# Layer 1's activations stored as they are, and turned by the loads that use them

## The chip, the cores and the metric

The kernel runs on one core of a Trainium2 chip. The metric is the device time of one execution in microseconds (us). Seven executions of the kernel before took 740.19 to 762.38 us, with a median of 745.99 us. The core has a matrix engine (TensorE: PE, its weight loads PEld), a vector engine (DVE), a scalar engine (ACT), a general engine (GpSimd: POOL), a queue processor (SyncE: SP) and 16 DMA engines, which all queues share. SP issues most transfers and takes its instructions in order; POOL issues others, among them most stores.

## The reference

The program computes a network of four blocks, A B A B, and all its gradients. A is a gated long convolution over the sequence, B a two-layer perceptron, each on a layernorm of its input with a residual around it; both A blocks and both B blocks share weights.

```python
def _B_ref(x, w1, w2):                       # S, D, F = 2048, 448, 1792
    h = jnp.einsum("bsd,df->bsf", x, w1)
    h = _silu(h)
    return jnp.einsum("bsf,fd->bsd", h, w2)

x = A_q
x = x + _A_ref(_layernorm(x), A_k, A_v, A_shift_k, A_ssm_k, A_ssm_D)
x = x + _B_ref(_layernorm(x), B_w1, B_w2)    # layer 1
x = x + _A_ref(_layernorm(x), A_k, A_v, A_shift_k, A_ssm_k, A_ssm_D)
x = x + _B_ref(_layernorm(x), B_w1, B_w2)    # layer 2
out, vjp = jax.vjp(f, A_q, A_k, A_v, A_shift_k, A_ssm_k, A_ssm_D, B_w1, B_w2)
return (out, *vjp(grad_out))
```

What matters here is the gradient of w2. It is the sum over both layers of a product over the sequence: activation (silu of h, 1792 features by 2048 positions) times the gradient that reaches the layer's output (2048 positions by 448).

## The kernel before, in words

The work has four stages, read from the trace's lines.

- **Prefix** (0 to about 100 us): the convolution of block A by a matrix form of the Fourier transform.
- **Main** (about 100 to 515 us), in chunks of 512 positions, four a layer. Layer 1 forward (to about 230 us); layer 2 forward and backward together (to about 400 us); layer 1 backward (to about 515 us).
- **Suffix** (about 515 us to the end): the backward convolution. It consists of small matmuls with vector work between them.
- **Weight-gradient jobs.** The gradients of w2 (`_gw2`) and w1 (`_gw1`) are cut into 14 blocks of 128 features each. A block is two jobs, one a layer, of 16 matmuls each (one for 128 positions), which add into one PSUM tile. A job (`_job`) first loads 128 features by 2048 positions (512 KB) into a tile dstat, in which 128 positions lie on the partitions. The jobs have no dependence on the work beside them, so their matmuls are put between other matmuls in a fixed order: `fill` does it in the layer-1 backward (about four jobs), `weave` in the suffix. Five buffers of dstat rotate (three in the layer-1 backward); a load is issued when the job that had the buffer is done.

In the forward, `h` computes a half chunk (7 of 14 feature blocks) of the hidden layer with features on the partitions: four PSUM groups, of which ACT writes silu to a tile aT and DVE or ACT a copy to dT. The tag of aT has three buffers: the aT of a half takes the buffer of the half three before it, and waits until everything that reads that one is done. `out` reads aT for the second matmul.

The w2 jobs need the activation turned, with positions on the partitions. Before the change this is done as follows.

- Layer 1, first half of a chunk: `store_turned` issues two transposing transfers on SP from aT into a tile "turned" (two buffers), 16 and 12 blocks of 128 by 128. The next call's `flush` issues the store of "turned" to A_d[0] in HBM.
- Layer 1, second half: blocks 4 to 6 of its seven likewise (12 blocks of 128 by 128). Blocks 0 to 3 go to AP_d untouched, by a store on POOL.
- Layer 2: both halves are turned and stored to A_d[1]. Besides, `turn_plain` in chunks 0 and 1 loads AP_d's four feature blocks back with a transposing transfer and stores them to A_d[0].
- The weights w2T and w1T, needed in the backward, are made by six transposing loads ("pieces"). From the fourth call of `store_turned` on, each call issues one behind its own transposes.
- The jobs of w2 then load from A_d[0] and A_d[1] with plain transfers (L891). The jobs of w1 load layer 2's part from GH_d, which was turned, and layer 1's part from GP_d, which was stored untouched, with a transposing load (L889).

The order of instructions on an engine comes from a scheduler, with places pinned by `issue_after`, `_in_turn` and `keep_in_program_order`. In the suffix, three transposing transfers on SP turn a part of the Fourier data (Zg<-A1g, L992); each is issued after the job load before it.

Lines that the prediction uses: L536 matmuls of `contract` (h and the backward's gh); L628 ACT's silu to aT; L113 a copy by DVE; L505 transposes of `store_turned`; L509 pieces; L512 and L523 stores to A_d; L522 `turn_plain`; L639 and L642 POOL's stores of dT and to AP_d; L889 and L891 loads of a job, L893 its matmuls; L1006 and L205 loads of kk_c and Minvs on POOL; L1148 small matmuls near the end.

Of the kernel before, what the change touches and what calls it, by code (L numbers as in the profile page):

```python
# [17 lines left out]
P = 128  # L18
# [4 lines left out]
NT = 16  # L23
# [97 lines left out]
def kernel(  # L121
# [36 lines left out]
    k.DT_d = dram.tile([4, 2, P, NF // 2, 512], BF16, name="DT_d")  # L158
    k.A_d = [dram.tile([P, NF, NT, P], BF16, name=f"A_d{i}") for i in range(2)]
    k.AP_d = dram.tile([4, P, S], BF16, name="AP_d")  # L160
    k.GH_d = dram.tile([P, NF, NT, P], BF16, name="GH_d")
# [36 lines left out]
    _ssm_suffix(k)  # L198


W2_PLAIN = (7, 8, 9, 10)

# [279 lines left out]
class Main:  # L482

    def __init__(self, k, es):
        self.k, self.nc, self.tc = k, k.nc, k.tc
        nc, tc = k.nc, k.tc
        pool = lambda name, **kw: es.enter_context(tc.tile_pool(name=name, bufs=1, reuse_waits="tile", **kw))
        self.wt = pool("mwt")
        self.w2T = self.wt.tile([P, ND, F], BF16, name="w2T")
        self.w1T = self.wt.tile([P, NF, D], BF16, name="w1T")  # L490
        self.td = pool("mtd")
        self.ch = pool("mch")
        self.X = k.X
        self.late = None
        self.turns = 0
        self.pieces = [(self.w2T[:, a:b, :], k.B_w2[:, lo:hi]) for a, b, lo, hi in ((0, 2, 0, 256), (2, 3, 256, 384), (3, 4, 320, 448))]
        self.pieces += [(self.w1T[:, a:b, :], k.B_w1[:, a * P:b * P]) for a, b in ((0, 5), (5, 10), (10, NF))]
        self.w1sb, self.w2sb, self.Y = k.w1sb, k.w2sb, k.Ysb

    def store_turned(self, dst, tile_, c, hh, groups=((0, 4), (4, 7))):  # L500
        nc = self.nc
        self.flush()
        an = self.td.tile([P, NF // 2, 4, P], BF16, name="turned", tag="S", bufs=2)
        for lo, hi in groups:
            nc.sync.dma_start_transpose(out=an[:, lo:hi].rearrange("p a t f -> p (a t) f"), in_=tile_[:, lo:hi, :].rearrange("p a s -> p (a s)"))  # L505
        self.turns += 1
        if self.turns > 3 and self.pieces:
            out, src = self.pieces.pop(0)
            i = nc.sync.dma_start_transpose(out=out, in_=src)  # L509
            self.tc.keep_in_program_order(i)  # L510
        lo, hi = groups[0][0], groups[-1][1]
        self.late = lambda: nc.sync.dma_start(out=dst[:, 7 * hh + lo:7 * hh + hi, 4 * c:4 * c + 4, :], in_=an[:, lo:hi])  # L512

    def flush(self):
        if self.late:
            self.late()
        self.late = None

    def turn_plain(self, i):
        an = self.td.tile([P, NT, P], BF16, name="turned", tag="S", bufs=2)  # L520
        self.flush()
        self.nc.sync.dma_start_transpose(out=an[:], in_=self.k.AP_d[i])  # L522
        self.late = lambda: self.nc.sync.dma_start(out=self.k.A_d[0][:, W2_PLAIN[i]], in_=an[:])  # L523

# [91 lines left out]
    def h(self, c, L, nT, half, hold, pre=None):  # L616
# [16 lines left out]
        if L == 1:  # L633
            if half == 1:
                with self.tc.issue_after(last.ins):
                    for _, d in hold:
                        self.slope(d)
        else:
            nc.gpsimd.dma_start(out=k.DT_d[c, half], in_=dT[:])  # L639
            self.store_turned(k.A_d[0], aT, c, half, ((0, 4), (4, 7)) if half == 0 else ((4, 7),))  # L640
            if half == 1:
                nc.gpsimd.dma_start(out=k.AP_d[:, :, 512 * c:512 * (c + 1)].rearrange("ft f s -> f ft s"), in_=aT[:, 0:4, :])  # L642
        if L == 1:
            self.store_turned(k.A_d[1], aT, c, half)
        return d0
# [26 lines left out]
    def ga(self, c, L, gT, dT, mid=None, loads=(None, None)):  # L672
# [3 lines left out]
        for fp in range(NF // 2):  # L676
# [15 lines left out]
            if fp in (3, 6):  # L692
# [3 lines left out]
                if L == 1:  # L696
                    self.store_turned(k.GH_d, ghT[hh], c, hh)
                else:
                    self.flush()
                    nc.gpsimd.dma_start(out=k.GP_d[7 * hh:7 * hh + 7, :, 512 * c:512 * (c + 1)].rearrange("ft f s -> f ft s"), in_=ghT[hh][:])  # L700
        return (ghT, *ld) if ld else ghT
# [74 lines left out]
    def run(self):  # L776
# [30 lines left out]
        for c in range(4):  # L807
# [4 lines left out]
            self.out(c, cur, True)  # L812
            if c < 2:
                self.turn_plain(2 * c)
                self.turn_plain(2 * c + 1)
            if c < 3:
# [64 lines left out]

def _job(k, ps, src, ft, mov, slot, start, stop, first=None):
    pl, tag, bufs = slot
    st = pl.tile([P, NT, P], BF16, name="dstat", tag=tag, bufs=bufs)
    with ExitStack() as es:
        if first is not None:
            es.enter_context(k.tc.issue_after(first))
        if src is None:
            k.job_load = k.nc.sync.dma_start_transpose(out=st[:], in_=k.GP_d[ft]).ins  # L889
        else:  # L890
            k.job_load = k.nc.sync.dma_start(out=st[:], in_=src[:, ft, :, :]).ins  # L891
# [5 lines left out]
def _gw2(k, pool, fts, slots, bufs=2, first=None):  # L897
    nc = k.nc
    for ft in fts:
        ps = k.psum.tile([P, 512], FP32, name="ps_d", tag="tr", bufs=2)  # L900
        for L, mov in ((0, k.X), (1, k.GO)):
            slot = slots.pop(0)
            slots.append(slot)
            yield from _job(k, ps, k.A_d[L], ft, mov, slot, L == 0, L == 1, first)
        o = pool.tile([P, D], BF16, name="dout", tag="dout", bufs=bufs)
# [4 lines left out]
def _gw1(k, pool, slots):  # L910
# [288 lines left out]
```

## Time and profile before

| what | value |
|---|---|
| median of 7 executions (lowest, highest) | 745.99 us (740.19, 762.38) |
| the profiled execution, and its span | 745.99 us, 744.2 us |
| granted TensorE clock, mean of the span | 0.993 |
| PE busy in the span; idle in 100:130, 130:160, 160:200, 200:400 | 697.5 us (94%); 2.3, 0.6, 3.3, 5.8 us |
| DMA engines, busy share in 100:130, 130:160, 160:200, 524:538, 538:558 | 0.78, 1.10, 1.13, 0.94, 1.11 |
| queue of SP (q1) | 112.71 MB, 63.2% of 16 engines' span |
| queue of POOL (q0) | 61.52 MB, 24.5% |
| turned<-aT, transposing, 28 times | median 6.4 us from issue to landing |
| dstat<-A_d, plain, 28 times | 5.2 us |
| dstat<-GP_d, transposing, 14 times | 7.1 us |

How to read it: all times on the page and in the trace are those of one profiled execution. A busy share of the DMA engines can pass 1, as packets overlap. "Landing" is the moment at which all 16 engines have reported a transfer done. A name like dstat<-A_d is the tile written and the one read. SP's time is that of issuing; a transposing transfer holds SP longer than a plain one, and longer still when the queues are full. In a list of waits, "A <- B" says that A's engine stood idle until B was done. The granted clock is the part of full speed that TensorE was given.

### The profile page before, as it was taken

To read this page: it belongs to the slowest core of one execution; us is meant where nothing else is said; L and a number is where in the kernel's file an instruction comes from. 1 tells how busy PE (TensorE), PEld (TensorE's weight loads), DVE (VectorE), ACT (ScalarE), POOL (GpSimd) and SP (SyncE) were. 2 spreads that over 40 slices of the span, in tenths; PEclk is the share of its full clock that TensorE was granted. 3 is DMA by queue.
4 is the path that set the end of the run, shared out by engine and by line. 5 is a ranking of instruction groups with operands and counts; after the bars stand their busy time and mean duration, and the time that the engine had idled before them with its cause. 6 is when DMAs were issued, how large, how long until landed. Compare 5 with 4: busy or idle time off the path is not lost.

```text
span 744.2 us, 12447 instructions
## 1 busy us (share of the span) xinstructions
PE 697.5 (94%) x4836; PEld 370.4 (50%) x4881; DVE 508.9 (68%) x1059; ACT 438.1 (59%) x555; POOL 118.5 (16%) x202
## 2 busy tenths in 40 slices
PE   6978789999899999999999999999999999999897
PEld 5866533444344443443434434434556667554453
DVE  4878888788633597885958979779218773697150
ACT  4688777666537578587686777755426675321001
POOL 1144222221100001000000100110201112233131
PEclk9999999999999999999999999999999999999999
DMA  9979959999999999888979845735896887999993
GB/s 312 235 191 273 358 186 240 214 289 238 287 221 256 210 204 276 196 219 187 229 197 272 300 180 208 288 108 172 295 291 251 319 314 237 306 251 220 216 222 72
DMA packets 200599, 177.55 MB, mean 239 GB/s; under 512 B 155162, under 2 KB 176734, under 8 KB 199388
## 3 DMA queue, kind: packets, MB, share of 16 engines
q1 hardware_dynamic: 184608, 112.71, 63.2%
q0 software_dynamic: 15008, 61.52, 24.5%
q10 hardware_dynamic: 924, 2.52, 1.0%
q8 instruction: 38, 0.62, 0.4%
q14 instruction: 21, 0.17, 0.1%
HBM read 69.32 MB, written 65.87 MB: 182 GB/s over the span
## 4 chain that ended last, share of the span: by engine, by line
PE 54%; DVE 16%; ACT 11%; DMA 10%; issue 4%; another core or an unknown queue 2%; SPq 1%; POOL 1%; ACTq 0%; DVEq 0%; POOLq 0%
PE ps_d L893 19%; PE ps_h L536 9%; PE ps_o L653 5%; PE ps_g L536 5%; PE ps_n L732 4%; DMA KB<-Z 4%; DMA turned<-aT 3%; DVE lb_junk L707 3%; DVE lb_u L718 2%; ACT nb L280 2%; PE ps_v L234 2%; PE ps_v L235 2%; ACT aT L628 1%; DVE dT L113 1%
## 5 line engine op out<-in xcount | busy, mean ns | idle before, releaser
L893 PEld LDWEIGHTS <-dstat 128*128 128x128 bf16 x896 | 85.3, 98 | 79.3 <-issue 4.5
L536 PE MATMUL ps_h<-nT,w1sb 128*128 128x512 bf16 (+1 forms) x432 | 103.6, 388 | 6.9 <-DVE dT L113 3.8
L536 PE MATMUL ps_g<-gT,w2T 128*128 128x512 bf16 (+1 forms) x432 | 94.3, 381 | 4.3 <-ACT ghp L682 3.1
L732 PE MATMUL ps_n<-w1T,ghT 128*128 128x448 bf16 x448 | 90.5, 353 | 0.9 <-DVE ghT L690 0.9
L653 PE MATMUL ps_o<-w2sb,aT 128*128 128x448 bf16 x448 | 91.2, 354 | 0.0
L893 PE MATMUL ps_d<-mov,dstat 128*128 128x448 bf16 x448 | 88.8, 356 | 1.5 <-DMA dstat<-GP_d 1.5
L628 ACT ACTIVATE aT<-ps_h 128x1024 bf16<-128x1024 f32 (+1 forms) x64 | 58.3, 916 | 49.1 <-PE ps_h L536 42.5
L113 DVE CAST dT<-ps_h 128x1024 bf16<-128x1024 f32 (+1 forms) x55 | 58.3, 1064 | 33.8 <-ACT aT L628 33.8
L536 PEld LDWEIGHTS <-w1sb 128*128 128x128 bf16 (+1 forms) x448 | 36.5, 97 | 69.8 <-issue 42.1
L536 PEld LDWEIGHTS <-w2T 128*128 128x128 bf16 (+1 forms) x448 | 35.2, 96 | 62.6 <-issue 30.3
L682 ACT CAST ghp<-ps_g 128x1024 bf16<-128x1024 f32 x56 | 55.6, 1005 | 16.7 <-PE ps_g L536 13.7
L732 PEld LDWEIGHTS <-ghT 128*128 128x128 bf16 x448 | 42.8, 98 | 40.8 <-DVE ghT L690 1.8
L653 PEld LDWEIGHTS <-aT 128*128 128x128 bf16 x448 | 41.9, 98 | 42.6 <-issue 5.0
L893 PE MATMUL ps_d<-X,dstat 128*128 128x448 bf16 x224 | 53.2, 353 | 0.2
L893 PE MATMUL ps_d<-GO,dstat 128*128 128x448 bf16 x224 | 51.7, 353 | 0.2
L944 ACT CAST dout<-ps_d 128x448 bf16<-128x448 f32 x14 | 7.4, 532 | 71.3 <-PE ps_d L893 63.7
L734 ACT ACTIVATE lb_u<-ps_n,rstd 128x448 f32<-128x448 f32 x32 | 20.3, 634 | 40.0 <-DVE X L719 15.5
L235 PEld LDWEIGHTS <-pb 128*128 128x128 bf16 x336 | 32.5, 98 | 9.8 <-DVE pb L454 6.4
L234 PEld LDWEIGHTS <-pa 128*128 128x128 bf16 x336 | 32.8, 98 | 7.2 <-DVE pa L453 4.3
L690 DVE TENSOR_TENSOR ghT<-dT,ghp 128x1024 bf16<-128x1024 bf16 (+1 forms) x32 | 19.5, 619 | 20.9 <-ACT ghp L682 20.8
L654 DVE TENSOR_TENSOR X<-X,ps_o 128x448 bf16<-128x448 bf16 x32 | 19.7, 615 | 15.3 <-PE ps_o L653 15.1
L613 ACT ACTIVATE dTl<-dTl 128x1024 bf16<-128x1024 bf16 (+1 forms) x32 | 29.8, 944 | 0.0
(207 smaller groups left out, 1181.1 us busy)
## 6 DMA issues: line engine op xcount, KB each, us to landing
dstat<-A_d SPq DMA_DIRECT2D x28, 512.0 KB, 5.2
A_d<-turned SPq DMA_DIRECT2D x12, 896.0 KB, 4.6
DT_d<-dT POOLq DMA_DIRECT2D x8, 896.0 KB, 8.7
GH_d<-turned SPq DMA_DIRECT2D x8, 896.0 KB, 5.0
dTl<-DT_d SPq DMA_DIRECT2D x8, 896.0 KB, 5.7
GP_d<-ghT POOLq DMA_DIRECT2D x8, 896.0 KB, 9.5
dstat<-GH_d SPq DMA_DIRECT2D x14, 512.0 KB, 4.5
spec_K<-Z POOLq DMA_DIRECT2D x7, 512.0 KB, 7.7
```

What stands on the lines that cost most here:

```text
L113: eng.tensor_copy(out, in_)
L234: nc.tensor.matmul(o, lhsT=pa[:, i * P:(i + 1) * P], rhs=k.Gsb[:, ga, :], start=True, stop=False)
L235: nc.tensor.matmul(o, lhsT=pb[:, i * P:(i + 1) * P], rhs=k.Gsb[:, gb, :], start=False, stop=True)
L536: self.nc.tensor.matmul(ps[:, u, :], lhsT=w[lo:hi, b, f:f + P], rhs=x[lo:hi, b, :], start=(seen[u] == 1), stop=(seen[u] == ND))
L613: self.k.last_slope = self.nc.scalar.activation(s, s, ACT.Derivative_silu)
L628: last = nc.scalar.activation(a, ps[:, 0:n, :], ACT.Silu)
L653: nc.tensor.matmul(po[:, :D], lhsT=aT[ft // 7][0][:, ft % 7, tl * P:(tl + 1) * P], rhs=self.w2sb[:, ft, :], start=(ft == 0), stop=(ft == N ...
L682: k.last_gh = nc.scalar.copy(gh[:], ps[:])
L707: nc.vector.scalar_tensor_tensor(out=junk[:], in0=u0, scalar=1.0, in1=n_t, op0=ALU.mult, op1=ALU.mult, accum_out=cp[:, 1:2])
L732: mm = nc.tensor.matmul(pn[:, :D], lhsT=ghT[ft // 7][:, ft % 7, tl * P:(tl + 1) * P], rhs=self.w1T[:, ft, :], start=(ft == 0), stop=(ft == ...
L734: last_u = nc.scalar.activation(u0[:], pn[:, :D], ACT.Identity, scale=k.rstd[2 * L + 1][:, t:t + 1], accum_out=cp[:, tl, 0:1])
L893: i = k.nc.tensor.matmul(ps[:, :D], lhsT=st[:, t, :], rhs=mov[:, t, :], start=start and t == 0, stop=stop and t == NT - 1)
```

## The change

Layer 1's activations are no longer turned in the forward. Each half's aT goes untouched to AP_d, now with room for all 14 feature blocks, by one store on SP (`store_plain`). POOL's four stores to AP_d and layer 2's `turn_plain` go. The pieces of w2T and w1T are issued by `next_piece`, one behind each layer-1 store from chunk 1 on, which is one half earlier than before. The layer-1 jobs of w2 load from AP_d with a transposing transfer, as the layer-1 jobs of w1 do from GP_d. Layer 2's own activations are turned and stored as before. PE, DVE and ACT have the same instructions in the same order; POOL has four fewer, SP 20 fewer.

```diff
-    k.A_d = [dram.tile([P, NF, NT, P], BF16, name=f"A_d{i}") for i in range(2)]
-    k.AP_d = dram.tile([4, P, S], BF16, name="AP_d")
+    k.A_d = dram.tile([P, NF, NT, P], BF16, name="A_d")
+    k.AP_d = dram.tile([NF, P, S], BF16, name="AP_d")
...
-W2_PLAIN = (7, 8, 9, 10)
...
-    def store_turned(self, dst, tile_, c, hh, groups=((0, 4), (4, 7))):
+    def store_turned(self, dst, tile_, c, hh):
         nc = self.nc
         self.flush()
         an = self.td.tile([P, NF // 2, 4, P], BF16, name="turned", tag="S", bufs=2)
-        for lo, hi in groups:
+        for lo, hi in ((0, 4), (4, 7)):
             nc.sync.dma_start_transpose(out=an[:, lo:hi].rearrange("p a t f -> p (a t) f"), in_=tile_[:, lo:hi, :].rearrange("p a s -> p (a s)"))
-        self.turns += 1
-        if self.turns > 3 and self.pieces:
+        self.late = lambda: nc.sync.dma_start(out=dst[:, 7 * hh:7 * hh + 7, 4 * c:4 * c + 4, :], in_=an[:])
+
+    def store_plain(self, eng, dst, tile_, c, hh):
+        eng.dma_start(out=dst[7 * hh:7 * hh + 7, :, 512 * c:512 * (c + 1)].rearrange("ft f s -> f ft s"), in_=tile_[:])
+
+    def next_piece(self):
+        if self.pieces:
             out, src = self.pieces.pop(0)
-            i = nc.sync.dma_start_transpose(out=out, in_=src)
-            self.tc.keep_in_program_order(i)
-        lo, hi = groups[0][0], groups[-1][1]
-        self.late = lambda: nc.sync.dma_start(out=dst[:, 7 * hh + lo:7 * hh + hi, 4 * c:4 * c + 4, :], in_=an[:, lo:hi])
+            self.tc.keep_in_program_order(self.nc.sync.dma_start_transpose(out=out, in_=src))
...
-    def turn_plain(self, i):
-        an = self.td.tile([P, NT, P], BF16, name="turned", tag="S", bufs=2)
-        self.flush()
-        self.nc.sync.dma_start_transpose(out=an[:], in_=self.k.AP_d[i])
-        self.late = lambda: self.nc.sync.dma_start(out=self.k.A_d[0][:, W2_PLAIN[i]], in_=an[:])
...
             nc.gpsimd.dma_start(out=k.DT_d[c, half], in_=dT[:])
-            self.store_turned(k.A_d[0], aT, c, half, ((0, 4), (4, 7)) if half == 0 else ((4, 7),))
-            if half == 1:
-                nc.gpsimd.dma_start(out=k.AP_d[:, :, 512 * c:512 * (c + 1)].rearrange("ft f s -> f ft s"), in_=aT[:, 0:4, :])
+            self.store_plain(nc.sync, k.AP_d, aT, c, half)
+            if c > 0:
+                self.next_piece()
         if L == 1:
-            self.store_turned(k.A_d[1], aT, c, half)
+            self.store_turned(k.A_d, aT, c, half)
...
             self.out(c, cur, True)
-            if c < 2:
-                self.turn_plain(2 * c)
-                self.turn_plain(2 * c + 1)
...
-def _job(k, ps, src, ft, mov, slot, start, stop, first=None):
+def _job(k, ps, src, ft, mov, slot, start, stop, first=None, plain=False):
...
-        if src is None:
-            k.job_load = k.nc.sync.dma_start_transpose(out=st[:], in_=k.GP_d[ft]).ins
+        if plain:
+            k.job_load = k.nc.sync.dma_start_transpose(out=st[:], in_=src[ft]).ins
...
-            yield from _job(k, ps, k.A_d[L], ft, mov, slot, L == 0, L == 1, first)
+            yield from _job(k, ps, k.A_d if L else k.AP_d, ft, mov, slot, L == 0, L == 1, first, L == 0)
...
-            for n, i in enumerate(_job(k, ps, k.GH_d if L == 1 else None, ft, mov, slot, L == 1, L == 0)):
+            for n, i in enumerate(_job(k, ps, k.GH_d if L else k.GP_d, ft, mov, slot, L == 1, L == 0, plain=L == 0)):
```

More of the change, by code (lines that the diff above doesn't have):

```diff
@@ L494, in __init__ @@
         self.late = None
-        self.turns = 0
         self.pieces = [(self.w2T[:, a:b, :], k.B_w2[:, lo:hi]) for a, b, lo, hi in ((0, 2, 0, 256), (2, 3, 256, 384), (3, 4, 320, 448))]
@@ L699, in ga @@
                     self.flush()
-                    nc.gpsimd.dma_start(out=k.GP_d[7 * hh:7 * hh + 7, :, 512 * c:512 * (c + 1)].rearrange("ft f s -> f ft s"), in_=ghT[hh][:])
+                    self.store_plain(nc.gpsimd, k.GP_d, ghT[hh], c, hh)
         return (ghT, *ld) if ld else ghT
```

## The prediction

> **What bounds the kernel now.** I read the page's totals first, then its slices, then the waits of TensorE, and last the two stretches of the trace that the change touches.
>
> ```profile
> span 744.2 us, 12447 instructions
> ...
> PE 697.5 (94%) x4836; PEld 370.4 (50%) x4881; DVE 508.9 (68%) x1059; ACT 438.1 (59%) x555; POOL 118.5 (16%) x202
> ...
> DMA  9979959999999999888979845735896887999993
> ```
>
> TensorE (PE) sets the time: 46.7 us of the span are all that it idles, 20 of them in the first 100 us, which the change doesn't touch. The order of the instructions on PE, DVE and ACT is the same in both kernels; SP and POOL alone differ. So the change can win only what PE now waits for a transfer, and lose only by making PE wait for one. The DMA engines are nearly full in most slices, so both can happen.
>
> *Where PE waits for the turning.* In the waits of all engines one line names the tile that is turned (total us, times, longest):
>
> ```profile
> ACT aT L628 <- DMA turned<-aT: 6.5, 1, 6.5
> ```
>
> The timeline there (start, length, engine, and in brackets the idle time before and what ended it):
>
> ```profile
> 188.77 1.51 ACT L628 ACTIVATE aT<-ps_h 128x512 bf16<-128x512 f32 x2 [6.46 <-DMA turned<-aT]
> 189.19 3.65 SPq L505 DMA_TRANSPOSE turned<-aT  x1
> 189.40 0.69 DVE L113 CAST dT<-ps_h 128x512 bf16<-128x512 f32 x1 [2.65 <-ACT aT L628]
> ...
> 190.14 0.71 PE L536 MATMUL ps_h<-nT,w1sb 64*128 64x512 bf16 x3 [2.50 <-DVE dT L113]
> ```
>
> Busy times of PE, PEld, DVE, ACT, POOL, then granted clock, DMA share and GB/s of the stretch 187 to 195:
>
> ```profile
> 187.00:195.00 8.00, 5.50 (x32) 3.08 (x31) 5.57 (x13) 4.26 (x5) 1.82 (x2) 0.79 1.14 268
> ```
>
> ACT may not write the buffer of aT (three in rotation) for chunk 3's second half before both transposes of chunk 2's first half have read it. That half was complete at 153.5; SP, which takes its queue in order, came to its transposes at 170.96 and 179.8, and they landed at 185.9 and 188.7. PE idles 2.5 us, and after it the granted clock is at half for 3.4 us: over these 8 us its mean is 0.79, 0.21 x 8 = 1.7 us lost. Together **4.2 us**. It is the only PE stall from 100 to 400 us above 1.3 us, and the only one put down to a transfer.
>
> *Where PE has little left.* The timeline of SP around the suffix's own transposes (Zg), and that of PE at its jobs 13 and 14:
>
> ```profile
> 524.67 4.86 SPq L891 DMA_DIRECT2D dstat<-A_d  x2
> 531.89 7.49 SPq L992 DMA_TRANSPOSE Zg<-A1g  x1
> 539.47 0.53 SPq L891 DMA_DIRECT2D dstat<-A_d  x1
> 540.05 4.44 SPq L992 DMA_TRANSPOSE Zg<-A1g  x1
> 544.58 0.53 SPq L891 DMA_DIRECT2D dstat<-A_d  x1
> 545.17 4.08 SPq L992 DMA_TRANSPOSE Zg<-A1g  x1
> ```
>
> ```profile
> 551.50 3.19 PE L893 MATMUL ps_d<-GO,dstat 128*128 128x448 bf16 x16
> 554.53 1.68 PE L893 MATMUL ps_d<-X,dstat 128*128 128x448 bf16 x8
> ```
>
> Number the dw2 jobs (16 matmuls each) from 0; the even ones are layer 1's. Issue / landing / first use in the trace: job 10: 524.7 / 528.5 / 540.6; job 12: 539.5 / 544.7 / 548.5; job 13: 544.6 / 549.4 / 551.5; job 14: 549.3 / 553.5 / 554.5; job 16: 550.4 / 556.3 / 563.8. What is left shrinks to 2.1 us at job 13 and **1.0 us at job 14**. Earlier jobs have 6.9 us or more, later ones 4.5 or more, and 15 to 21 from job 18 on.
>
> **The change, part by part.**
>
> *Layer-1 forward, SP.* Twelve transposes (160 blocks of 128x128) and eight stores to A_d go, eight stores of 896 KB to AP_d come. The store reads aT as soon as the half is done, not 17 us later behind a queue of transposes; stores of that size on this queue land in a median 4.6 us (A_d<-turned). Landing near 158 to 165 and not 188.7, it leaves ACT free at 185.9, when PE's first group of that half is ready. Next late there are ACT's normalizations, done at 182.3, still ahead of PE. So the stall goes, and with it the half clock: **-4.2 us**. Bounds: 0 (the stall stays) and -4.2; no other PE wait of this stage names a DMA.
>
> *Weight pieces.* w2T and w1T go out one half earlier, each behind a store. First use of w2T is at 230.8; the last w1T piece now lands at 225.5. Nothing: covered by 20 us or more.
>
> *POOL.* Four stores to AP_d go (0.77 us of issue each). POOL is 16% busy and nothing on PE's path waits for them: 0.
>
> *Layer 2, SP.* Four transposes from AP_d and four 512 KB stores go (230 to 291 us). The idle of PE from 200 to 400 us, 5.8 us, is put down to ACT and DVE (ghp, nb, nT, lb_u), not to a transfer: 0, at most -0.5.
>
> *dw2 jobs.* Fourteen of 28 loads become transposing loads of the same 512 KB from AP_d; the trace has this form as dstat<-GP_d. In numbers of SP: 1.3 to 10.6 us of issue and not 0.32. In the layer-1 backward (jobs 0, 2, 4) SP stands idle from 406.5 to 412.9 before its next load, and these jobs have 11.5 us and more. Loads 6 and 8, issued by 501, are used at 525 and 533. What matters are the transposing loads 10, 12 and 14, which stand in SP's queue, and in the DMA rings, ahead of job 14's first matmul.
>
> What one costs more than a plain load, in full-DMA time: alone on the engines a plain load fills a share of 0.45 of 4.1 us (519.9 to 524), 1.85 us; a transposing one 0.94 of 2.9 us (700.4 to 703.3), 2.7. Difference 0.85. With queues full: plain loads land 1.3 us apart (555.1, 556.3, 557.6), and a Zg transpose of the same 16 blocks with a plain load behind it takes 4.7 and 4.1 us (544.7, 549.4, 553.5), so 3.1 for the transpose, difference 1.8. The lower end is none, if the engines' pauses near 528 take it up. I take 0.85, since part of the 3.1 is the change from a transpose to a plain load, and here transpose follows transpose. Then 3 x 0.85 = 2.6: job 14 lands at 556.1, 1.6 after PE wants it. Job 13 lands at 549.4 + 1.7 = 551.1, just in time. A PE stall of 1.6 us keeps the clock (the 1.6 us gap at 682 did; those of 2.5 and 2.8 at 187 and 690 did not): **+1.6 us**. Afterwards PE takes 5.9 us for a job and the loads get ahead again.
>
> The Trainium skill (DMA: Bandwidth & Descriptors, Latency and other measured facts) gives transposes an effective 261 GB/s, against 341 GB/s for 1 MB of plain load in its table of measured bandwidth: an estimate of 2.0 and 1.5 us for 512 KB. By that page the three would cost 1.4 us, the stall 0.4, and the sum would be 742.2; the trace's rows are both longer, so they are used.
> The same page (Queues, rings and completion order) has each engine take turns between queues packet by packet, which speaks against this change, as a transpose's packets are small: in the rows above the first Zg transpose held SP for 7.49 us beside POOL's loads, the next two 4.4 and 4.1. By that rule load 10 could sit until about 540 behind POOL's loads, just ahead of its use at 540.6.
>
> **Sum**, against the profiled execution (745.99; 744.2 of span and 1.8 around it): 745.99 - 4.2 + 1.6 = **743.4 us**. That execution is also the median of the seven shown, of which three lie near 740 to 741.5 and two at 754 and 762. A measurement of this kernel can hardly tell less than 1% from no change.
>
> **Rivals.**
> 1. *The cover holds.* Loads 10, 12 and 14 fit into pauses and PE never waits: 745.99 - 4.2 = 741.8. For it: PE wants job 14 only 1.6 us before my landing. Against: the DMA share is 0.94 from 524 to 538 and 1.11 from 538 to 558.
> 2. *Slower: the loads starve.* One mechanism: at 526 to 541 POOL loads four kk_c of 512 KB and Minvs of 1 MB, and then the Zg transposes queue; the three loads pay the full-queue price, 1.8 each. Job 14 lands 5.4 later, the stall is 4.4, the clock drops (1.7): 745.99 - 4.2 + 6.1 = 747.9. It decides where one transposing load costs more than (1.0 + 2.5) / 3 = 1.2 us extra: then the stall passes 2.5, and with the clock eats the 4.2. The loads from GP_d at 630 to 681 speak for it (up to 17.9 us to landing, SP held 10.6). With the worst of these, one at 12.1 - 5.2 = 6.9 and two at 1.9 (medians 7.1 and 5.2), the stall is 9.7: 753.2.
> 3. *The stall at 187 doesn't go.* The weight pieces stand on SP between the stores; one of them took 13.5 us to land. If a store is as late as the transposes were, 745.99 + 1.6 = 747.6. Against: the half is ready 32 us before its buffer is wanted.
> 4. *More than the sum.* The second gap with a clock drop (2.8 + 1.7 us at 690) is of no transfer that the profile names; if it shrinks with other timing, 738.9.
>
> **How the numbers follow.** Forecast 0.42, rival 1 0.2, rival 2 0.2 (0.06 of it over 753), rival 3 0.08, rival 4 0.1. The predicted time is 743.4. The range leaves out the ends of 2 and 4 and takes in the scatter of the runs at the low end: 738 to 751. Under 738.5 lies most of rival 4 and some of rival 1, as the fastest runs before are 740.2: 0.15. Over 753.5, the worst of rival 2 with the long runs: 0.15. Within 1%: 0.70.
>
> **What would show it.** Right: no wait of ACT aT for a DMA, no half clock near 190, PE's ps_h of that half without a gap over 0.6 us; ahead of 530 all PE times about 4 us earlier; then one PE gap of 1 to 2.5 us at the start of ps_d<-X near 551, its releaser a DMA dstat<-AP_d. Wrong: that gap above 2.5 with a clock of one half behind it (rival 2), or none (rival 1); a gap left before 200 (rival 3); PE waits for dstat<-AP_d before 515 or after 565, which I price at nothing.

## The result

The change makes the kernel slower. Before, 64 executions had a median of 746.29 us; after, 27 had 758.29 us (741.81 to 782.21). The ratio is **1.0125, 95% interval 1.0088 to 1.0162**, some 9.3 us of 746; the medians are 12.0 us apart. (A ratio compares only the executions near each kernel's fastest and a median holds all of them, so the two can differ.) The profiled execution of after took 749.88 us, against 745.99 for that of before.

The page of after; in the slices 40 stand for the span, 18.7 us each:

```profile
span 748.1 us, 12403 instructions
...
PE 698.8 (93%) x4836; PEld 373.4 (50%) x4881; DVE 508.2 (68%) x1059; ACT 438.3 (59%) x555; POOL 115.3 (15%) x198
...
PE   5988879999999999999999999999999599999997
...
PEclk9999999999999999999999999999999889999999
DMA  9879957999865967768989953956999997999994
GB/s 289 231 174 274 341 217 270 181 210 340 212 128 148 198 173 176 174 170 202 217 213 252 344 186 130 307 133 171 302 244 295 150 278 248 312 289 268 250 220 72
```

PE does what it did (697.5 us before). One slice sticks out, the 32nd, from 580 to 598 us: PE is busy for half of it, and the clock is lower there and in the next. The DMA engines are marked as full in that slice, yet they moved 150 GB/s, against 295 and 278 in its neighbours.

Stage by stage, as busy time of PE, PEld, DVE, ACT, POOL, granted clock, DMA share and GB/s. First before:

```profile
160.00:200.00 40.00, 36.71 (x188) 16.44 (x191) 29.86 (x61) 24.41 (x31) 8.31 (x12) 0.96 1.13 269
575.00:605.00 30.00, 29.84 (x306) 20.98 (x307) 22.73 (x41) 20.99 (x23) 6.89 (x13) 1.00 0.80 297
640.00:700.00 60.00, 55.70 (x485) 29.10 (x484) 43.13 (x74) 10.97 (x15) 16.99 (x34) 0.97 1.14 239
```

and after:

```profile
160.00:200.00 40.00, 38.90 (x208) 17.31 (x210) 31.92 (x70) 27.65 (x35) 7.94 (x10) 1.00 0.93 232
575.00:605.00 30.00, 20.77 (x191) 14.25 (x191) 12.25 (x22) 12.47 (x15) 3.75 (x8) 0.83 1.10 188
640.00:700.00 60.00, 60.00 (x539) 33.13 (x537) 43.27 (x60) 14.44 (x19) 17.30 (x35) 1.00 1.12 277
```

In 160 to 200 PE gained 2.2 us of busy time and 0.04 x 40 = 1.6 us of clock: 3.8. In 575 to 605 it lost 9.1 us and 0.17 x 30 = 5.1 us of clock: 14.2. In 640 to 700 it gained 4.3 and 1.8: the gap at 690 is small in this execution. The sum, 4.3 us lost, is about the difference of the spans (3.9). Leaving out the gap at 690, which comes and goes from run to run (experiment 1 had 3.5 us of it), 14.2 - 3.8 = 10.4 us, close to the 9.3 of the ratio. The size of the loss varies from execution to execution, as the experiments show, so that closeness proves little.

What PE waited for in the slow stretch, from the waits of PE (total us, times, longest), and what the instruction that it waited for was waiting for, from the page's groups:

```profile
PE ps_v L231 <- DVE pa L1027: 8.8, 1, 8.8
```

```profile
L1027 DVE TENSOR_TENSOR pa<-Zg,kk_c 128x1024 bf16<-128x1024 bf16 x28 | 19.3, 689 | 20.1 <-DMA kk_c<-spec_KV 16.5
```

kk_c is a piece of the spectrum that the suffix multiplies by. POOL loads it, from tensors that the change doesn't touch. The timeline of POOL there (start, length of the issue, in brackets the idle time before):

```profile
574.00 0.53 POOL L995 DMA_DIRECT2D kk_c<-spec_K  x1 [6.94 <-DVE pb L1028]
574.52 0.53 POOL L996 DMA_DIRECT2D kk_c<-spec_KV  x1
575.34 0.55 POOL L896 DMA_DIRECT2D out_dram<-dout  x1 [0.29 <-PE ps_v L231]
575.89 0.53 POOL L1003 DMA_DIRECT2D gks<-in_A_v_dram  x1
583.05 0.53 POOL L995 DMA_DIRECT2D kk_c<-spec_K  x1 [6.63 <-DVE pb L1028]
...
603.98 0.53 POOL L995 DMA_DIRECT2D kk_c<-spec_K  x1 [15.36 <-DVE pb L1028]
```

and of SP:

```profile
574.12 4.04 SPq L878 DMA_TRANSPOSE dstat<-AP_d  x1
579.80 0.32 SPq L880 DMA_DIRECT2D dstat<-A_d  x1
586.47 16.38 SPq L878 DMA_TRANSPOSE dstat<-AP_d  x1
603.59 0.77 SPq L880 DMA_DIRECT2D dstat<-A_d  x1
```

At 574 a transposing job load and POOL's loads set out together: kk_c (two of 512 KB), a small store, and gks (1.75 MB, in rows of 14 KB). The DMA view of 570 to 610 of after has the rate by the microsecond, and the issues with KB each and median us to landing:

```profile
GB/s 461 414 463 379 350 320 324 267 277 169 166 147 65 119 99 106 67 110 122 93 102 135 133 41 199 177 418 345 311 241 264 191 175 240 204 169 362 348 410 393
...
gks<-in_A_v_dram POOLq DMA_DIRECT2D x1, 1792.0 KB, 26.2
...
kk_c<-spec_KV POOLq DMA_DIRECT2D x3, 512.0 KB, 21.7
...
dstat<-AP_d SPq DMA_TRANSPOSE x3, 22.5
```

Before, the same view has:

```profile
kk_c<-spec_KV POOLq DMA_DIRECT2D x4, 512.0 KB, 6.2
gks<-in_A_v_dram POOLq DMA_DIRECT2D x1, 1792.0 KB, 10.9
```

From 582 to 594 some 100 GB/s moved. The stretch 579 to 595, in the columns of the stages, first before and then after:

```profile
579.00:595.00 16.00, 15.89 (x161) 11.06 (x162) 11.98 (x23) 11.05 (x13) 2.65 (x5) 1.00 0.81 317
```

```profile
579.00:595.00 16.00, 9.76 (x95) 6.51 (x94) 2.98 (x6) 7.86 (x9) 1.60 (x3) 0.91 1.09 117
```

A third of the rate at a higher busy share: the engines are occupied, but by packets that take long. On POOL's queue a 4 KB packet takes 159 ns as a rule (the median of this execution), but from 580 to 595 one in ten took 4.1 us or more, the longest 6.4. On SP's queue the seven plain ones of that stretch took a median of 4.7 us. The kk_c that PE's next work needs, issued at 574.5, landed at 596.8; with the 6.2 us of before it would have been about 581:

```profile
588.27 0.54 PE L882 MATMUL ps_d<-X,dstat 128*128 128x448 bf16 x2
596.88 0.69 DVE L1027 TENSOR_TENSOR pa<-Zg,kk_c 128x1024 bf16<-128x1024 bf16 x1 [14.12 <-DMA kk_c<-spec_KV]
...
597.63 0.29 PE L231 MATMUL ps_v<-Gs,pa 128*128 128x128 bf16 x1 [8.81 <-DVE pa L1027]
```

PE stands for 8.8 us, and the granted clock is at half from 592.0 to 602.2, which is another 5.1.

### The profile page after: what moved, and what is told of

It reads as the page before. It is cut to its first block, busy times and chain, and to the rows that moved or that the text cites. A ratio compares the mean times of both kernels' runs of the same rounds, so it can differ in the third digit from the quotient of the medians.

```text
span 748.1 us, 12403 instructions
## 1 busy us (share of the span) xinstructions
PE 698.8 (93%) x4836; PEld 373.4 (50%) x4881; DVE 508.2 (68%) x1059; ACT 438.3 (59%) x555; POOL 115.3 (15%) x198
## 4 chain that ended last, share of the span: by engine, by line
PE 46%; DVE 20%; ACT 9%; issue 4%; DMA 3%; another core or an unknown queue 2%; POOL 1%; ACTq 0%; DVEq 0%; POOLq 0%
PE ps_d L882 18%; PE ps_h L528 7%; PE ps_o L645 6%; PE ps_g L528 5%; PE ps_n L724 4%; DVE lb_junk L699 3%; DMA kk_c<-spec_KV 3%; DVE dT L113 3%; DVE lb_u L710 3%; ACT nb L277 2%; DVE lb_u L742 1%; ACT na L277 1%; PE ps_v L232 1%; PE ps_v L231 1%
## 5 line engine op out<-in xcount | busy, mean ns | idle before, releaser
L528 PE MATMUL ps_h<-nT,w1sb 128*128 128x512 bf16 (+1 forms) x432 | 101.2, 381 | 4.7 <-DVE dT L113 1.6
L882 PE MATMUL ps_d<-mov,dstat 128*128 128x448 bf16 x448 | 87.2, 352 | 0.0
L645 PEld LDWEIGHTS <-aT 128*128 128x128 bf16 x448 | 41.9, 98 | 42.6 <-issue 5.0
L231 PEld LDWEIGHTS <-pa 128*128 128x128 bf16 x336 | 34.0, 101 | 16.5 <-DVE pa L1027 9.3
L231 PE MATMUL ps_v<-Gs,pa 128*128 128x128 bf16 x224 | 29.3, 223 | 8.8 <-DVE pa L1027 8.8
L1027 DVE TENSOR_TENSOR pa<-Zg,kk_c 128x1024 bf16<-128x1024 bf16 x28 | 19.3, 689 | 20.1 <-DMA kk_c<-spec_KV 16.5
```

The source lines that it names most:

```text
L231: nc.tensor.matmul(o, lhsT=pa[:, i * P:(i + 1) * P], rhs=k.Gsb[:, ga, :], start=True, stop=False)
L528: self.nc.tensor.matmul(ps[:, u, :], lhsT=w[lo:hi, b, f:f + P], rhs=x[lo:hi, b, :], start=(seen[u] == 1), stop=(seen[u] == ND))
L645: nc.tensor.matmul(po[:, :D], lhsT=aT[ft // 7][0][:, ft % 7, tl * P:(tl + 1) * P], rhs=self.w2sb[:, ft, :], start=(ft == 0), stop=(ft == N ...
L882: i = k.nc.tensor.matmul(ps[:, :D], lhsT=st[:, t, :], rhs=mov[:, t, :], start=start and t == 0, stop=stop and t == NT - 1)
```

## The experiments

The theory after the result: a transposing load from HBM, in flight beside the loads of another queue, slows both many times over (**collision**). Its rivals: the transposing work as such fills the DMA engines (**work**), and SP, held up by the transposes, comes late to what stands behind them (**queue**). Where a line of code is not shown, the kernel is that of after.

### 1. The layer-1 loads plain

```diff
-            k.job_load = k.nc.sync.dma_start_transpose(out=st[:], in_=src[ft]).ins
+            k.job_load = k.nc.sync.dma_start(out=st[:].rearrange('p t f -> p (t f)'), in_=src[ft]).ins
```

(for layer 1 of the w2 jobs)

> The change, with layer 1's loads of the w2 jobs plain instead of transposing: same source AP_d, same 512 KB, same place in SP's queue. It leaves out the turning of layer 1's activations, so the gradient of w2 lacks it. If the transposing loads cost the time (all theories that blame them): no PE gap of 9 us near 590, no load of kk_c over 12 us to landing, and only the gain of the forward is left, 4 us under the kernel before: ratio 0.990 to 0.998. If the untouched stores of the forward cost it: still 1.01 to 1.015.

Measured: ratio 0.9999 (0.9961 to 1.0038), 740.92 us median of 12. No gap of PE near 590; kk_c landed in 4.0 to 9.1 us. So the cost comes from the loads and not from the stores. And without them the forward's part is worth nothing that the ratio shows, where I had expected 0.990 to 0.998.

### 2. The transposing loads alone

The forward and layer 2 of the kernel before, with an added copy of layer 1's activations from which the jobs load with transposing transfers:

```diff
+    k.A_0 = dram.tile([NF, P, S], BF16, name="A_0")
+    k.A_d[0] = k.A_0[:].rearrange("ft p (t f) -> p ft t f", f=P)
...
+        if plain:
+            k.job_load = k.nc.sync.dma_start_transpose(out=st[:], in_=src[ft]).ins
```

(the data are turned twice, so layer 1's share of the gradient of w2 is another quantity)

> The kernel before with its whole forward (turned there, stored turned), but layer 1's loads of the w2 jobs transposing, from a tensor of AP_d's layout. It turns layer 1's activations twice, so the gradient of w2 is not the reference's. If the transposing loads cost the time: kk_c waits and a PE gap of 5 to 11 us between 575 and 605 come with them, without the forward's gain: ratio 1.012 to 1.025. If the stores cost it: 1.00.

Measured: ratio 1.017 (1.0111 to 1.0228), 758.09 us median of 6. PE waits 13.2 us in one piece for pa behind kk_c of spec_KV (26.6 us to landing), and the clock is at half for 17.1 us. The loads alone bring the whole cost. Against after, the forward of before costs 0.0045 of 746, or 3.4 us, but the two intervals overlap.

### 3. POOL's loads into SP's queue

```diff
-                nc.gpsimd.dma_start(out=t[0], in_=k.SPEC_d["K"][:, lo:hi])
-                kv = nc.gpsimd.dma_start(out=t[1], in_=k.SPEC_d["KV"][:, lo:hi])
+                q = nc.gpsimd if cp < 2 else nc.sync
+                q.dma_start(out=t[0], in_=k.SPEC_d["K"][:, lo:hi])
+                kv = q.dma_start(out=t[1], in_=k.SPEC_d["KV"][:, lo:hi])
...
-                        nc.gpsimd.dma_start(out=gks[:], in_=v_pm)
+                        nc.sync.dma_start(out=gks[:], in_=v_pm)
```

(likewise ksf and mov3)

> The change, with the suffix's loads of kk_c from the third pair on, of ksf, gks and mov3 issued by SP instead of POOL, so that they stand in one queue with the transposing loads. Same bytes, same number of transposes. Collision theory (a transposing load from HBM and a load of another queue slow each other several times over while both are in flight): no packet phase at a quarter of the rate, kk_c lands within 12 us, PE has no gap over 3 us between 575 and 605; ratio 0.990 to 1.002. Work theory (the transposes simply fill the DMA engines): kk_c is as late as in the change, ratio 1.008 to 1.016. Queue theory (SP is held by the transposes' issue): worse than the change, over 1.013, as kk_c now stands behind them.

Measured: ratio **0.9978 (0.9947 to 1.0009)**, 740.7 us median of 12. The transposing loads are all there, only now they and the other loads follow each other in one queue. The DMA view of 560 to 600:

```profile
kk_c<-spec_KV SPq DMA_DIRECT2D x5, 512.0 KB, 5.5
...
gks<-in_A_v_dram SPq DMA_DIRECT2D x1, 1792.0 KB, 11.3
...
dstat<-AP_d SPq DMA_TRANSPOSE x4, 9.1
```

The same bytes, the same transposes, and gks takes 11.3 us and not 26.2. From 571 to 600 the engines moved 310 GB/s; with all job loads plain (experiment 1) it was 323. The work theory falls, and the queue theory too, since SP has more in its queue here than anywhere.

### 4. Feature blocks 11 and 12 plain, twelve transposing

```diff
-            yield from _job(k, ps, k.A_d if L else k.AP_d, ft, mov, slot, L == 0, L == 1, first, L == 0)
+            yield from _job(k, ps, k.A_d if L else k.AP_d, ft, mov, slot, L == 0, L == 1, first, ('as is' if ft in (11, 12) else True) if L == 0 else False)
```

> The change, with two of the fourteen loads (feature blocks 11 and 12, issued near 574 and 586) plain; it leaves out the turning of these two blocks. Collision theory: these are the two in flight beside POOL's large loads, so the whole PE gap near 590 goes: ratio 0.990 to 1.000. Work theory: 2 of 14 of the cost goes, ratio 1.008 to 1.014.

Measured: ratio 0.9983 (0.9948 to 1.0017), 740.35 us median of 12; kk_c in 4.0 to 9.6 us; no gap near 590. Two of fourteen transposing loads carry the cost.

### 5. The reverse: only those two transposing

The same line, with `('as is' if ft not in (11, 12) else True)`.

> The change with transposing loads only for the two feature blocks 11 and 12; the other twelve layer-1 jobs load plainly what was never turned, so this kernel leaves the turning of those twelve blocks out. The collision theory (a transposing load in flight beside POOL's loads of kk_c and gks slows both): those two are the transposing loads that fly there, so two of fourteen carry the whole cost: kk_c of spec_KV takes over 15 us to land, PE stands for 5 to 9 us near 589 us, and the time stands 0.8 to 2% above the kernel before's. The work theory (fourteen transposes cost DMA time wherever they stand): two sevenths of a seventh at most, a time within 0.3% of that with all loads plain, and kk_c landing in 4 to 8 us.

Measured: ratio 1.0166 (1.0105 to 1.0228), 752.28 us median of 6. The DMA view of 565 to 612, and the waits of PE:

```profile
gks<-in_A_v_dram POOLq DMA_DIRECT2D x1, 1792.0 KB, 37.9
...
kk_c<-spec_KV POOLq DMA_DIRECT2D x2, 512.0 KB, 33.5
...
dstat<-AP_d SPq DMA_TRANSPOSE x2, 34.7
```

```profile
PE ps_v L231 <- DVE pa L1029: 20.4, 1, 20.4
```

Both sides of the pair are met: without these two no cost, with these two alone all of it. The size is not fixed: 20.4 us of standing in this execution, 8.8 in that of after.

### 6. Transfers by themselves

Nothing but transfers of some 0.5 MB, in phases of six of each kind, with a barrier between them. `turn` is a transposing load of 512 KB from HBM on SP, `load` a plain one of 448 KB, `end` the barrier:

```diff
+    for i in range(N):
+        turn(i)
+        load(nc.gpsimd, i)
+    end()
```

> Only transfers, in phases with a barrier between them; the whole computation is left out. Alone, a transposing load of 512 KB from HBM should take about 2.7 us of all DMA engines, as in the trace, and a plain one 1.9. The collision theory: with transposing loads and POOL's loads of kk_c's and gks's kind in flight together, the phase takes well over the sum of the two alone (over 1.5 times), and both plain queues together take about their sum. If the collapse is of the two queues, the phase in which both kinds stand in one queue takes about the sum; if it is of the transposing and reading packets at the same DMA engine, that phase is slowed as well. With the transposed source in SBUF, or with POOL storing in place of loading: over 1.5 times the sum if any second queue does it, about the sum if the reads from HBM do it. The work theory: every phase takes about the sum of its parts.

Stretches of the transposing loads alone, the plain ones alone, and both in two queues (POOL, clock, DMA share, GB/s):

```profile
12.80:30.20 17.40, 0.04 (x1) 1.00 0.94 181
30.20:40.50 10.30, 3.15 (x6) 1.00 0.72 267
40.50:66.90 26.40, 3.18 (x6) 1.00 1.01 223
```

17.4 + 10.3 = 27.7, and both together took 26.4: the sum, no collapse. With the source in SBUF, 25.1; with stores in place of loads, 22.8; in one queue, 26.1; with the plain loads on ACT's queue, 25.7. With SP's six loads plain as well, in two queues, the phase took 16.9: here a transposing load cost (26.4 - 16.9) / 6 = 1.6 us more than a plain one. My expectation missed: a transposing load beside any plain load is not enough.

### 7. gks earlier, on SP

```diff
-                        nc.gpsimd.dma_start(out=gks[:], in_=v_pm)
+                        nc.sync.dma_start(out=gks[:], in_=v_pm)
```

> The change with the one load of gks (1.75 MB) issued by SP in place of POOL, ahead of the transposing loads of the last layer-1 jobs; kk_c stays on POOL. If the collision needs the large load as its partner: kk_c lands in 4 to 9 us, no gap of PE over 2 us near 589, time 0.990 to 1.002 of the kernel before. If the small loads of kk_c (a quarter to half a megabyte each) beside the transposing loads are enough: kk_c still takes over 12 us, and the time stays 0.8 to 1.7% above the kernel before's.

Measured: ratio 1.0061 (1.0022 to 1.0099), 743.96 us median of 12. The gap near 589 is gone, with kk_c of spec_KV there in 11.7 us. That is over the 4 to 9 that I had expected, and the ratio lies above my 0.990 to 1.002: SP now issues gks at 525.4, and the loads of jobs 10 to 16 come late behind it. The waits of PE:

```profile
PE ps_d L882 <- DMA dstat<-AP_d: 3.1, 2, 2.0
PE ps_d L882 <- DMA dstat<-A_d: 2.8, 1, 2.8
```

The large load has a part in the collapse, and the place with little slack, where the prediction looked, does exist: it takes 1.75 MB ahead of it to run out.

### 8. The slow stretch's own set of transfers

Again transfers only: on SP a transposing, a plain and a transposing load (T, p, T), on POOL two kk_c, a store, gks, two kk_c, all by their real shapes.

> Only transfers again, the whole computation left out, now with the set that flew in the slow stretch: two transposing loads and a plain one of 512 KB on SP, and on POOL four loads of 512 KB in rows of 4 KB, a store, and one load of 1.75 MB in rows of 14 KB; then the same set with one thing changed at a time. If the set of transfers is enough for the collapse: the full set takes 25 us or more where the same with plain loads takes 11 to 13 (some 4.7 MB at 410 KB per us), and leaving the large load out, or splitting it into four, brings it to its volume's worth. If the engines' own work on SBUF is needed, the full set takes 12 to 16 us alone and 25 or more in the phase in which VectorE and ScalarE work beside it. If neither, all phases take their volume's worth (within some 4 us of the plain set), and what is needed is something that this set leaves out.

Measured, in us for a phase: full set 30.9 and, again at the end, 27.9; with plain loads 18.4; without gks 16.0; without the store 18.9; gks on ACT's queue 20.2; gks in four pieces 24.6; POOL's set on ACT's queue 41.9; with VectorE and ScalarE at work 25.9, and plain with them 18.3 to the last landing. For the plain set I had expected 11 to 13, from 4.7 MB; seven loads of 512 KB, gks and the store are 6.1 MB. All but the full set ran once, so the values between 16 and 20 settle nothing by themselves (experiments 11 and 13 repeat some). But the set of transfers that collapses is there twice, and once more in ACT's queue. So the set of transfers is enough. The other engines' accesses to SBUF are not needed, nor is POOL's way of issuing.

### 9 and 10. gks in four pieces; gks later

```diff
-                        nc.gpsimd.dma_start(out=gks[:], in_=v_pm)
+                        for j0 in range(0, J, 4):
+                            nc.gpsimd.dma_start(out=gks[:, j0:j0 + 4, :], in_=v_pm[:, j0:j0 + 4, :])
```

> The change with the load of gks in four loads of rows of 3.5 KB on the same queue at the same place; bytes and order are those of the change, and the instructions of the other engines too. If the long rows (packets of 14 KB beside the transposing load's 256 B) make the collapse: kk_c lands in 4 to 10 us, no gap of PE over 3 us near 589, time 0.993 to 1.003 of the kernel before's. If the volume in flight in two queues does: kk_c takes over 15 us, PE stands for 5 us or more, 1.008 to 1.02.

```diff
-                    if cp == 3:
-                        nc.gpsimd.dma_start(out=gks[:], in_=v_pm)
                     if cp == NCI // 2 - 1:
                         nc.gpsimd.dma_start(out=k.mov3[:], in_=_pm(k.N_d[3][:]))
+                        nc.gpsimd.dma_start(out=gks[:], in_=v_pm)
```

> The change with the load of gks at the end of POOL's list of this stage (after mov3, some 38 us later), when the last of the layer-1 transposing loads has landed; it is first used at 651 us, 30 us later. All other instructions keep their order. If the large load is the partner that the collapse needs: kk_c lands in 4 to 9 us, no gap near 589, time 0.992 to 1.000 of the kernel before's, as with all loads on SP. If kk_c's loads beside the transposes are enough: over 12 us to landing and 1.008 to 1.02.

In pieces: ratio 1.0103 (1.0046 to 1.016), PE waits 8.9 us, kk_c up to 23.3 us. It is not the length of the rows. Later: ratio **1.0003 (0.9942 to 1.0064)**, 744.46 us median of 12; no gap near 589, and kk_c:

```profile
DMA to landing us min/median/max: 4.0/5.3/13.3
```

The 13.3 is over the 9 that I had expected, and 16 us of this stretch run at 232 GB/s: kk_c alone beside the transposing load still slows, but not beyond what PE has in hand. In that trace gks is issued at 600.7 and not at 575.9, just after the last of the three transposing loads of this stretch has landed (600.5). One large load, moved back within its queue, takes the cost away, as far as an interval of 0.6% either way can tell.

### 11 and 12. Does the store have a part?

One more set of transfers, with a store of 112 KB as in the kernel; and the kernel with four of the stores on ACT:

```diff
-        nc.gpsimd.dma_start(out=k.outs[8][ft * P:(ft + 1) * P, :], in_=o[:])
+        (nc.scalar if ft in (8, 9, 10, 11) else nc.gpsimd).dma_start(out=k.outs[8][ft * P:(ft + 1) * P, :], in_=o[:])
```

> Only transfers, the whole computation left out: the set of the slow stretch once more, now with a store of 112 KB as in the kernel, its phases a change at a time, and the full set, the set with plain loads and the set without a store run twice. By volume (some 5.5 MB) the plain set should take 16 to 18 us, and the two transposing loads 2 us more. If store, large load and transposing loads are all needed: the full set takes 24 us or more, and without the store, with the store on another queue, or with a load in its place 17 to 21 us. If the store has no part in it: these three take 24 us or more like the full set, and what brought the earlier phase without a store to 18.7 us was chance.

> The change with four of the stores of dout (feature blocks 8 to 11, 112 KB each) issued by ScalarE behind the copy that fills them, in place of POOL; the loads stay where the change has them. If the store ahead of the large load in POOL's queue is needed for the collapse: kk_c lands in 4 to 10 us, no gap of PE over 3 us near 589, time 0.993 to 1.003 of the kernel before's. If the transposing load and the large load in two queues are enough: kk_c takes over 15 us and the time stays 1.006 to 1.02 of the kernel before's.

Transfers, in us: full set 30.2 and 24.5; plain 16.3 and 16.0; without the store 18.4 and 24.5; store after gks 18.8, ahead of all 20.1, on ACT 24.4; a load in its place 26.8; one transposing load and two plain ones 36.0; two transposing loads and no plain one 17.0 with the store, and 16.9 without it. The kernel: ratio 1.0143 (1.0088 to 1.0197), PE waits 16.6 us. The store is not needed. The 18.9 and 18.4 without it were chance, as the second go shows: the plain set repeats within 0.3 us, the mixed ones don't repeat at all.

### 13. The same phases, four times each

> Only transfers, the whole computation left out: seven phases, each run four times in turn, so that chance and rule can be told apart. Plain set (three loads of 512 KB on SP; on POOL four of 512 KB and the large one): 15 to 17 us every time. With the first and third SP load transposing: if any transposing load beside the large load is enough, 18 us or more every time, and as much for two transposing loads without a plain one behind, and for a single one. If a plain load queued behind the transposing one in the same queue is needed: 24 us or more at least half the time with it (also for one transposing load and a plain one behind), and 14 to 18 us every time where none stands behind it. Without the large load 14 to 17 us by both. All in the one queue of SP: 17 to 20 us by volume if it takes two queues; the transfers alone cannot be slower there than in two queues by either.

| SP's queue (T transposing, p plain) | POOL's queue | us in four goes |
|---|---|---|
| p, p, p | 4 kk_c, gks | 15.7, 16.3, 15.9, 16.1 |
| T, p, T | 4 kk_c, gks | 31.7, 22.9, 27.3, 32.4 |
| T, T | 4 kk_c, gks | 25.6, 26.0, 21.0, 29.3 |
| T, p | 4 kk_c, gks | 16.5, 16.9, 18.8, 21.9 |
| T | 4 kk_c, gks | 21.3, 22.0, 15.5, 15.2 |
| T, p, T | 4 kk_c | 16.8, 14.2, 15.9, 16.4 |
| T, p, T and 4 kk_c, gks, all on SP | | 18.0, 18.1, 18.1, 17.9 |

The first go of the first, second, sixth and last row in the trace:

```profile
28.20:43.90 15.70, 2.60 (x5) 1.00 0.87 351
43.90:75.60 31.70, 2.60 (x5) 1.00 1.04 174
...
138.90:155.70 16.80, 2.08 (x4) 1.00 0.99 218
155.70:173.70 18.00, 0.00 (x0) 1.00 0.91 306
```

In one queue the set costs 2.0 us more than with plain loads in two (the plain set in one queue was not run), about what two transposing loads add in the work that the prediction priced (2 x 0.85 = 1.7), and it does so every time. In two queues it costs 7 to 16 us more, by chance. A plain load behind the transposing one isn't needed (third row), which the 17.0 and 16.9 of experiment 11 had left open. One transposing load is enough in half of the goes; I had expected 18 us or more every time, so that missed. Without gks the phase loses less: its 3.7 MB took 14.2 to 16.8 us, where at the 351 GB/s of the plain set they would take 10.5 (an estimate; that set was not run all plain). What happens inside the DMA engines, and what decides how bad one go gets, no run here shows.

## Why the prediction was wrong, step by step

**Forward, -4.2 us: the step came true in the profile, but its size was that of one execution.** PE's busy time and clock in 160 to 200 rose by 3.8 us together, there is no half clock near 190, and ACT no longer waits for a DMA before aT. The sign that PE would be about 4 us earlier ahead of 530 did not come: job 14 began only 1.3 us earlier (553.20 and 554.53), as PE of after was already 3.9 us later at the layernorm's transposes ahead of the first half chunk (103.66 and 99.81), which the change doesn't touch. And the stall is not the same in each execution of the old forward: experiment 2, which has it, stood for 1.6 us near 200 and had no half clock. Four executions of the kernel before are on record with a mean granted clock of 1.000 (736.08, 736.74, 736.77 and 737.17 us); one half clock of 3.4 us would make it 0.998, so there the 1.7 us were not there to be won. Kernels with the new forward and without the collision (1, 3, 4, 10) have ratios of 0.998 to 1.000. No run shows a gain in time from this step.

**Weight pieces, POOL's stores, layer 2: 0.** PE's busy time in 200 to 420 is 212.48 us, before 212.49. But the pieces, now issued earlier, came to fly beside other transfers too: the three of w2T took 17.4 to 23.3 us to land, before 6.2 to 13.5. Their first use at 229.5 left them time. The stores beside them had less: in experiment 4 one to AP_d took 24.0 us and landed at 172.59, ACT's next write of aT began at 172.70, and PE stood for 1.8 us near 175; in experiment 7 one took 22.9 us, and ACT waited 2.3 us for it, without harm to PE. That this is the same collision was not tested.

**The dw2 jobs, +1.6 near 551: the place was right, the size was 0.3.** The page's group of layer 1's job matmuls, with the idle time before them at the end:

```profile
L882 PE MATMUL ps_d<-X,dstat 128*128 128x448 bf16 x224 | 54.2, 358 | 0.4 <-DMA dstat<-AP_d 0.3
```

Load 14 landed at 553.2, just as PE wanted it. Three transposes cost the queue less there than 2.6 us, as rival 1 had it.

**What failed is the sentence "Afterwards PE takes 5.9 us for a job and the loads get ahead again", and with it the price of nothing after 565.** It is true of the job loads: job 22, landing after 24.9 us, still wasn't missed. The step asked of each transposing load only when it itself would land. It did not ask what else was in flight beside it. From job 18 on I took the 15 to 21 us in hand as cover, and didn't list the loads of another queue there, whose users have far less: kk_c is issued when its buffer comes free, at 574.5, and DVE wanted it 8.2 us later (it idles 14.12 us up to 596.88). Those loads pay for a transposing load beside them, and with gks beside both the price was 14.2 us in the profile.

**Rival 2 had half of it.** It had the direction, the kind of mechanism (loads starving beside POOL's loads) and the clock that drops after it. It had the wrong stretch (526 to 541, where the loads did no harm) and the wrong victim. That its worst case, 753.2, is nearer to 745.99 x 1.0125 = 755.3 than the forecast is luck: it is a sum over other loads. Rival 4 came true in the profiled execution (the gap at 690, 4.3 and 1.8 us in 640 to 700), but that gap was back with 3.5 us in experiment 1.

**The trace had a hint that I read too narrowly.** I quoted loads from GP_d that took 17.9 us to land and the first Zg transpose, 7.49 us beside POOL's loads, and used both as prices of the transposing load itself. With the stages of before beside them (busy share 1.14 at 239 GB/s in 640 to 700, where transposing loads fly, and 0.80 at 297 GB/s in 575 to 605, where none do) they could have been read as a sign that two queues together move less, and so as a price on the other queue.

On the page of the Trainium skill that the prediction weighed (DMA: Bandwidth & Descriptors): its section Queues, rings and completion order, by which each DMA engine takes turns between queues packet by packet, would, with the trace's packets of 256 B and 14 KB, have made the transposing load starve and gks do well. The runs show both slow, gks from 10.9 to 26.2 us. That page's Rules for kernel authors say that a transpose next to ordinary DMAs needs nothing. There the matter is the data; as to time, two queues cost 23 to 32 us here where one took 18. The page states its 261 GB/s, which the prediction took for transposes at large, for a non-contiguous middle dimension; in experiment 6 six transposing loads alone moved 181 GB/s, their latency included.

**The clock.** I had set the point from which it drops between idle stretches of 1.6 and 2.5 us. Experiment 1 stood for 3.5 us at 689 and experiment 7 for 2.8 near 548 with the clock at full, while before lost it after 2.5. The length alone does not decide. The clock's changes lie on a grid of 3.41 us (see the last section). Laid on it, the step that lost the clock held 2.0 us of idle time (before, from 188.1) and 2.85 (from 689.9); the steps that kept it held at most 1.8 (experiment 1) and 1.9 (experiment 7). That is no rule yet: in before a step from 99.4 with 1.7 us lost it too. And the gap at 682, which I had at 1.6 us, is 1.46 in the trace.

## What to carry to other kernels

When a plain transfer becomes a transposing one, list what the other queues have in flight at each of its places, and ask how long their users can wait, not only its own. Here two of fourteen transposing loads, beside one load of 1.75 MB in another queue, carried the whole cost, as far as the ratios can tell. The cures are an order: the large load later (ratio 1.0003), or the loads that fly together in one queue (0.9978 of the kernel before; against the change as it was made 0.9978 / 1.0125 = 0.9855, an estimate from two ratios). A DMA share near 1 says nothing about throughput (0.87 stood for 351 GB/s and 1.04 for 174 in experiment 13); read it with the GB/s beside it.

## What the runs showed of the hardware that I had not expected

- Two transposing loads of 512 KB from HBM with a plain one on SP, beside four plain loads of 512 KB and one of 1.75 MB in another queue, moved 174 GB/s where the same set all plain moved 351; in the kernel it was about 100, with a busy share of 1.0 or more. Single 4 KB packets in the kernel then took up to 6.4 us where 159 ns is the rule, and the time of the set varies from go to go (23 to 32 us). In one queue the penalty is gone (17.9 to 18.1). Beside loads of 448 KB alone (experiment 6) there was none: 26.4 us, the sum.
- It isn't of POOL's queue: with the second set on ACT's queue the one go took 41.9 us. Nor of the rows' length: in four pieces 24.6 us, and in the kernel a ratio of 1.0103.
- The half clock comes in whole steps: 10.2, 17.1 and 20.5 us after the long gaps, 3, 5 and 6 times 3.41. In each trace its changes after the first stand on one grid of that step. The Trainium skill (TensorE: Matmul & The Clock Gate, part 1) has a free-running window of 3.4 us, and the grid in this case's traces agrees. It would explain why a gap's place in the window can matter as much as its length, as the idle time by steps above suggests.
